# Sliding-window attention, two layers on one core: score units of two head groups by 256 queries, DMA transposes, bank pairs given out by the scheduler

## The chip, the core and the metric

The kernel runs on one NeuronCore of a Trainium2 chip. The core's engines work side by side, each in the order of its own instruction list: PE (TensorE, matmuls, with PEld its weight loads), ACT (ScalarE), DVE (VectorE), POOL (GpSimd) and SP (SyncE, which here only issues DMAs). PE writes to PSUM, eight banks of 512 f32 columns in 128 partitions; the other arrays lie in SBUF. The metric is the device time of one execution in microseconds.

## What is computed

x is 2048 rows of 512 (bf16). Two layers follow each other, each an attention block and a block that updates one row:

```python
x = x + A(layernorm(x))          # H = 32 heads of 16, window W = 256
    qkv = x @ wqkv
    scores = q k^T / 4; mask: 0 <= query - key < 256
    o = softmax(scores) v;  A = o @ wo
x = x + B(layernorm(x))          # B(x) = x + upd
    r = x @ w_r; idx = argmax(r)          # one row of 2048
    y = (silu(x[idx] @ w_gate) * (x[idx] @ w_up)) @ w_down
    upd[idx] = y * sigmoid(r[idx])
```

## The kernel before

The rows are worked on in tiles of 128, 16 a layer; both layers are one stream of 32 tiles, T = 0 to 31. Every operation is entered into a list with its engine, its reads and writes, an assumed duration and a priority (in units of a tile: `at` = T plus a fraction), and `Sched.schedule` plays the list through with these durations and writes down one fixed order for each engine. On the chip each engine follows its order and waits on semaphores; nothing is reordered there.

The steps of the stream, with their lines in the profile:

- `ln` makes the normalized tile XN (statistics on DVE, L516 and L517; the rest on POOL, L519 to L529), which PE transposes in eight pieces into PSUM (L546) and DVE copies to XNT (L554).
- For each batch of four tiles `qk` makes Q and K transposed for four groups of eight heads (L584; copies to QT and KTN, L603 and L605), and `vproj` makes V of each tile (L620, copy to VN, L627).
- `kscat` spreads K by eight DMAs for two tiles into the block-diagonal KBD (L639), `vscat` sends V through DRAM (`vd`, L648) into VBD by four DMAs (L654). These, the loads of x and the stores of the rows (`scr`, `out`) stand in SP's queue in the scheduled order.
- `attention` works on one tile of 128 keys. A unit is one of four head groups `s` by one of four blocks of 32 keys by the 288 queries that these keys can meet: two matmuls on the two halves of PE's rows, one for each bank of a pair (L682, four heads in each), then two small matmuls that add the mask, -30000, to the first and last 32 queries of the bank (L688), then one exponential on ACT over 2 x 288 columns into PT (L696). Units alternate between two bank pairs.
- The same function multiplies PT by VBD, with a column of ones for the denominators (L716, 192 matmuls a tile), into the pair ACC; DVE takes the reciprocal (L729, one a tile) and writes the normalized tile ON (L734).
- `out_proj` of tile T stands with tile T + 1: PE transposes ON (L546), DVE copies it to OT (L554), PE multiplies by WO (L750), DVE adds the residual (L755), and `mod_tile` makes the second normalization, the router value and the stores.
- All matmuls but the scores and PV share one pair, MISC.
- `select`, after 11 tiles of layer 0 and 12 of layer 1, finds the row: DVE reduces in each partition (L828 to L833), a DMA writes 128 pairs to DRAM (`vcd`, L834) and another reads them back into all partitions (BC, L835), DVE goes on (L837 to L848), then three DMAs gather the row. `mlp_gu` (L916) and `mlp_down` (L954) are its three products; the weights are loaded to MW in chunks of 0.9 MB. Whether the early choice held is checked at the end; where it did not, a second, plain kernel runs (it does not run here).

The pairs, and how a group is bound to one, are fixed in the code:

```python
ACC = 4
MISC = 6
...
                pair = 2 * (i % 2)
```

Of the kernel before, what the change touches and what calls it, by code (L numbers as in the profile page):

```python
# [56 lines left out]
class _Op:  # L57
    __slots__ = ("idx", "eng", "fn", "deps", "dur", "name", "is_dma", "prio", "signals", "count",
                 "dma_sem", "start", "end", "waits", "dma_extra", "force")

    def __init__(self, idx, eng, fn, deps, dur, name, is_dma, prio):
        self.idx = idx
        self.eng = eng
        self.fn = fn
        self.deps = deps
        self.dur = dur
        self.name = name
        self.is_dma = is_dma
        self.prio = prio
        self.signals = False  # L70
        self.count = 0
# [5 lines left out]
        self.force = None  # L77


class Sched:  # L80
# [6 lines left out]
    def __init__(self, dma_latency=2000.0, sem_latency=100.0, n_dma_slots=48):  # L87
# [7 lines left out]
        self.dma_ops = []  # L95
        self.base = 0.0
        self._vc_lookup = {}

    def add(self, eng, fn, reads=(), writes=(), banks=(), dur=100.0, name="", is_dma=False, prio=None, extra_deps=()):
# [13 lines left out]
        for b in banks:  # L113
# [11 lines left out]
        self.ops.append(op)  # L125
        for k in writes:
# [8 lines left out]
    def dma(self, queue, fn, reads=(), writes=(), nbytes=0, name="", prio=None, extra_deps=(), dur=None):  # L135
# [5 lines left out]
        op.dma_extra = nbytes / 150.0  # L141
# [8 lines left out]
    def schedule(self):  # L150
        ops = self.ops
        n = len(ops)
        users = [[] for _ in range(n)]
# [7 lines left out]
        for op in ops:  # L161
            if remaining[op.idx] == 0:
                _heappush(now[op.eng], (op.prio, op.idx))
        t_eng = {e: 0.0 for e in self.ENGS}
        order = {e: [] for e in self.ENGS}
        done = 0
        while done < n:
# [33 lines left out]
            done += 1  # L201
            for u in users[i]:
                remaining[u] -= 1
                uo = ops[u]
                rt = op.end + (self.sem_latency if self.needs_wait(uo, op) else 0.0)
                if rt > ready_time[u]:
                    ready_time[u] = rt
                if remaining[u] == 0:
                    ue = uo.eng
                    if ready_time[u] <= t_eng[ue]:  # L210
                        _heappush(now[ue], (uo.prio, u))
                    else:
                        _heappush(fut[ue], (ready_time[u], uo.prio, u))
# [16 lines left out]
    def analyze(self):  # L230
# [23 lines left out]
        while done < total:  # L254
# [12 lines left out]
            assert progressed, "deadlock in schedule order (cyclic wait)"  # L267

# [31 lines left out]
    def run_engine(self, e, handle, sems, dma_sems):  # L300
# [13 lines left out]
        if e == "sp":  # L314
# [5 lines left out]
            for slot, tot in sorted(totals.items()):  # L320
                handle.wait_ge(dma_sems[slot], tot)


ACC = 4
MISC = 6
NBATCH = 4
NS1 = 11
# [4 lines left out]
W = 288  # L332
# [3 lines left out]
class Builder:  # L336
# [16 lines left out]
    def alloc(self):  # L353
# [11 lines left out]
        self.XNT = self.sb("XNT", [128, 2, 4, 512], BF16)  # L365
# [11 lines left out]
        self.ONESB = self.sb("ONESB", [128, 128], BF16)  # L377
        self.ZEROB = self.sb("ZEROB", [128, 64], BF16)
        self.IDB = self.sb("IDB", [128, 128], BF16)
        self.II = self.sb("II", [128, 128], BF16)  # L380
        self.BM = self.sb("BM", [128, 2, 32], BF16)
# [15 lines left out]
        self.EQ = self.sb("EQ", [128, 128], F32)  # L397
        self.CAND = self.sb("CAND", [128, 128], F32)
        self.VC = self.sb("VC", [128, 2], F32)
        self.BC = self.sb("BC", [128, 128, 2], F32)  # L400
# [16 lines left out]
        self.VCD = nc.dram_tensor("vcd", [2, 128, 2], F32)  # L417
        self.uctr = 0
# [15 lines left out]
    def init(self):  # L434
# [12 lines left out]
        S.dma("act", lambda e: e.dma_start(self.WO[:], self.A_wo.rearrange("(kc p) n -> p kc n", p=128)), writes=["wo"], nbytes=512 * 1024, name="ld_wo", prio=-7.0)  # L447
# [4 lines left out]
        S.add(P, lambda e: e.memset(self.ONESB[:], 1.0), writes=["onesb"], dur=100)  # L452
        S.add(P, lambda e: e.memset(self.MHALF[:], -0.5), writes=["mhalf"], dur=60)
        S.add(P, lambda e: e.affine_select(out=self.IDB[:], in_=self.ONESB[:], pattern=[[-1, 128]], compare_op=ALU.is_equal,
                                           fill=0.0, base=0, channel_multiplier=1), reads=["onesb"], writes=["idb"], dur=300)
        S.base = -8.0
        S.add(P, lambda e: e.affine_select(out=self.M8[:], in_=self.ONESB[:, 0:8].rearrange("p (a h) -> p a h", a=2), pattern=[[-64, 2], [-16, 4]],
                                           compare_op=ALU.is_ge, fill=0.0, base=0, channel_multiplier=1), reads=["onesb"], writes=["m8"], dur=100)
# [3 lines left out]
        S.add(P, lambda e: e.memset(self.ZEROB[:], 0.0), writes=["zerob"], dur=100)  # L462
        S.add(P, lambda e: e.memset(self.II[:], 0.0), writes=["ii"], dur=100)
        S.add(P, lambda e: e.memset(self.BM[:], 0.0), writes=["bm"], dur=100)
        r = slice(0, 32)
        S.add(P, lambda e: e.affine_select(out=self.II[r, :].rearrange("p (a b) -> p a b", a=4), in_=self.ONESB[r, :].rearrange("p (a b) -> p a b", a=4),
                                           pattern=[[0, 4], [1, 32]], compare_op=ALU.is_equal, fill=0.0, base=0, channel_multiplier=-1),
              reads=["onesb"], writes=["ii"], dur=200)
        S.add(P, lambda e: e.affine_select(out=self.BM[r, 0, :], in_=self.ZEROB[r, 0:32], pattern=[[1, 32]], compare_op=ALU.is_ge,
# [1606 lines left out]
```

## Time and profile before

| | |
|---|---|
| runs (median, lowest, highest) | 434.2 us, 433.31, 435.35 |
| profiled execution | 433.42 us, of it 431.7 between first and last instruction |
| mean granted TensorE clock | 0.906 |
| first tile's reciprocal to the last's | 44.3 to 411.1 us |
| exponentials L696, 128x576 | 448, mean 651 ns |
| score matmuls L682, 128x288 | 896 |
| mask matmuls L688 | 1024 |
| PV matmuls L716 | 5760 |
| transposes L546 | 512 pieces of 64 columns |

A group's row names line, engine, operation, tiles and shape, then busy time and the mean of one instruction, then the engine's idle time just before them and what ended it. A mean holds an instruction's latency, part of which overlaps with its neighbours; for PE above all, spacing is read from starts in the timeline. In a row of the waits stand who waited, for whom, the us in total, the number of waits and the longest.

### The profile page before, as it was taken

To read this page: it belongs to the slowest core of one execution; us is meant where nothing else is said; L and a number is where in the kernel's file an instruction comes from. 1 tells how busy PE (TensorE), PEld (TensorE's weight loads), DVE (VectorE), ACT (ScalarE), POOL (GpSimd) and SP (SyncE) were. 2 spreads that over 40 slices of the span, in tenths; PEclk is the share of its full clock that TensorE was granted. 3 is DMA by queue.
4 is the path that set the end of the run, shared out by engine and by line. 5 is a ranking of instruction groups with operands and counts; after the bars stand their busy time and mean duration, and the time that the engine had idled before them with its cause. 6 is when DMAs were issued, how large, how long until landed. Compare 5 with 4: busy or idle time off the path is not lost.

```text
span 431.7 us, 22240 instructions
## 1 busy us (share of the span) xinstructions
PE 354.1 (82%) x10109; PEld 246.1 (57%) x10109; DVE 227.5 (53%) x551; ACT 295.8 (69%) x526; POOL 152.5 (35%) x373
## 2 busy tenths in 40 slices
PE   0598898799899999698699978899999998739862
PEld 0254566567666676457655556666766677517620
DVE  6773564347546655556355575466544555404441
ACT  2257788778988898765285858777988788845400
POOL 9963044324424352234314074243522132312040
PEclk9999999899999999989569999989999999956555
DMA  8704124222453233337741924423442243750600
GB/s 269 254 13 92 31 46 114 26 91 46 105 93 95 69 99 60 83 83 232 225 87 29 317 40 123 98 103 79 101 81 72 59 99 70 198 127 5 197 14 21
DMA packets 107023, 43.69 MB, mean 101 GB/s; under 512 B 82980, under 2 KB 101285, under 8 KB 106920
## 3 DMA queue, kind: packets, MB, share of 16 engines
q1 hardware_dynamic: 105432, 40.74, 36.5%
q8 instruction: 81, 1.33, 1.3%
q10 hardware_dynamic: 1488, 1.44, 1.1%
q14 instruction: 22, 0.18, 0.1%
HBM read 24.26 MB, written 13.96 MB: 89 GB/s over the span
## 4 chain that ended last, share of the span: by engine, by line
PE 53%; ACT 15%; DMA 10%; DVE 7%; SPq 6%; issue 5%; POOL 3%; DVEq 0%; ACTq 0%; POOLq 0%
ACT PT L696 14%; PE PS L584 13%; PE PS L682 11%; PE PS L716 9%; PE PS L750 7%; PE PS L620 6%; DMA vcd<-VC 4%; SPq L639 4%; PE PS L954 2%; DVE XR L755 2%; PE PS L688 2%; DMA KBD<-KTN 2%; DMA BC<-vcd 2%; PE PS L546 2%; PE PS L916 1%
## 5 line engine op out<-in xcount | busy, mean ns | idle before, releaser
L696 ACT ACTIVATE PT<-PS 128x576 bf16<-128x576 f32 (+5 forms) x512 | 287.0, 621 | 85.8 <-PE PS L688 82.4
L682 PE MATMUL PS<-QT,KBD 64*128 64x288 bf16 (+6 forms) x1024 | 146.6, 291 | 27.9 <-ACT PT L696 17.8
L716 PE MATMUL PS<-VBD,PT 64*128 64x34 bf16 x5760 | 116.2, 176 | 7.1 <-issue 4.4
L716 PEld LDWEIGHTS PS<-VBD,PT 64*128 64x128 bf16 x5760 | 97.5, 94 | 18.4 <-issue 10.2
L688 PE MATMUL PS<-BM,II 64*128 64x64 bf16 (+1 forms) x1024 | 100.5, 194 | 2.7 <-issue 2.7
L682 PEld LDWEIGHTS PS<-QT,KBD 64*128 64x128 bf16 x1024 | 52.0, 96 | 66.0 <-ACT PT L696 40.5
L777 POOL TENSOR_SCALAR RSM<-XR 128x1 f32<-128x1 f32 x32 | 9.3, 292 | 208.5 <-DVE XR L772 208.4
L584 PE MATMUL PS<-XNT,WQKV 64*128 64x512 bf16 x512 | 69.3, 396 | 3.3 <-DVE VN L627 2.2
L688 PEld LDWEIGHTS PS<-BM,II 64*128 64x128 bf16 x1024 | 52.4, 98 | 9.3 <-issue 2.2
L750 PE MATMUL PS<-WO,OT 64*128 64x256 bf16 x512 | 44.9, 300 | 2.0 <-DVE OT L554 0.7
L603 DVE CAST QT<-PS 128x512 bf16<-128x512 f32 x28 | 19.4, 692 | 48.5 <-PE PS L584 48.5
L755 DVE TENSOR_TENSOR XR<-PS,XR 128x512 f32<-128x512 f32 x32 | 22.1, 692 | 41.3 <-PE PS L750 39.9
L620 PE MATMUL PS<-WQKV,XNT 64*128 64x256 bf16 x512 | 40.4, 277 | 2.2 <-DVE XR L755 1.6
L584 PEld LDWEIGHTS PS<-XNT,WQKV 64*128 64x128 bf16 x512 | 22.0, 97 | 26.3 <-issue 4.2
L627 DVE CAST VN<-PS 128x512 bf16<-128x512 f32 x32 | 22.1, 692 | 15.3 <-PE PS L620 12.5
L750 PEld LDWEIGHTS PS<-WO,OT 64*128 64x128 bf16 x512 | 21.9, 102 | 11.4 <-DVE OT L554 2.6
L620 PEld LDWEIGHTS PS<-WQKV,XNT 64*128 64x128 bf16 x512 | 20.9, 95 | 10.7 <-DVE XR L755 3.4
L529 POOL TENSOR_SCALAR XN<-XR,RS 128x512 bf16<-128x512 f32 (+1 forms) x28 | 21.5, 769 | 10.1 <-PE PS L546 9.4
L605 DVE CAST KTN<-PS 128x512 bf16<-128x512 f32 x28 | 19.0, 678 | 10.8 <-DMA KBD<-KTN 10.8
L554 DVE COPY XNT<-PS 128x512 bf16<-128x512 bf16 x32 | 13.5, 421 | 21.2 <-PE PS L546 21.0
L734 DVE TENSOR_TENSOR ON<-PS,RD 128x256 bf16<-128x256 f32 x64 | 24.1, 414 | 0.4
L546 PE MATMUL PS<-IDB,XN 64*128 64x64 bf16 x256 | 10.0, 201 | 15.7 <-ACT XN L526 14.2
(101 smaller groups left out, 310.0 us busy)
## 6 DMA issues: line engine op xcount, KB each, us to landing
scr<-XR SPq DMA_DIRECT2D x13, 516.0 KB, 4.3
vd<-VN SPq DMA_DIRECT2D x16, 272.0 KB, 3.5
VBD<-vd SPq DMA_DIRECT2D x64, 68.0 KB, 2.8
XR<-scr SPq DMA_DIRECT2D x8, 512.0 KB, 4.4
KBD<-KTN SPq DMA_DIRECT2D x120, 32.0 KB, 2.9
MW<-in_B_w_gate_dram SPq DMA_DIRECT2D x4, 896.0 KB, 7.0
MW<-in_B_w_down_dram SPq DMA_DIRECT2D x4, 896.0 KB, 5.7
XR<-in_A_x_dram SPq DMA_DIRECT2D x8, 256.0 KB, 6.9
```

Of the source, the lines that this page charges most:

```text
L529: S.add("pool", lambda e: e.tensor_scalar(out=XN[:, k2, :], in0=x, scalar1=RS[:, k4, 1:2], scalar2=RS[:, k4, 2:3], op0=ALU.mult, op1=ALU.add),
L584: r = e.matmul(self.PS[:, bank + w, :], lhsT=self.WQKV[rows, j, 512 * w + 128 * s:512 * w + 128 * s + 128], rhs=XNT[rows, kb, j, :], start ...
L603: S.add("dve", lambda e: e.tensor_copy(out=self.QT[:, s, tok], in_=self.PS[:, MISC, :]), banks=[MISC], writes=["qt%d_%d" % (b % 4, s)], du ...
L620: r = e.matmul(o, lhsT=XNT[rows, kb, j, 128 * jt:128 * jt + 128], rhs=self.WQKV[rows, j, 1024 + 256 * w:1280 + 256 * w], start=(ph == 0 an ...
L627: S.add("dve", lambda e: e.tensor_copy(out=vout, in_=vin), banks=[MISC, MISC + 1], writes=["vn%d_%d" % (pr % 2, m2)], dur=650, name="evv")
L682: r = e.matmul(self.PS[:, pair + x, 0:n], lhsT=self.KBD[rows, k2, s, 4 * (T % 2) + b, :], rhs=self.QT[rows, s, q0:q0 + n], start=True, sto ...
L688: r = e.matmul(o, lhsT=self.II[rows, :], rhs=w, start=False, stop=True, skip_group_check=True)
L696: return e.activation(out=o, in_=self.PS[:, pair:pair + 2, 0:n], func=ACTF.Exp, scale=0.25)
L716: r = e.matmul(self.PS[:, ACC + x, 34 * gg:34 * gg + 34], lhsT=self.PT[rows, c:c + 128], rhs=self.VBD[rows, v3, b8, :, gg, :], start=st, s ...
L734: S.add("dve", lambda e, o=o, i0=i0, i1=i1: e.tensor_tensor(out=o, in0=i0, in1=i1, op=ALU.mult), reads=["rd%d" % t], banks=[ACC + x], writ ...
L750: r = e.matmul(self.PS[:, MISC + w, 0:256], lhsT=self.OT[rows, k2, j, :], rhs=self.WO[rows, j, 256 * w:256 * w + 256], start=(ph == 0 and ...
L755: S.add("dve", lambda e: e.tensor_tensor(out=self.xf(T).rearrange("p (x c) -> p x c", x=2), in0=self.PS[:, MISC:MISC + 2, 0:256], in1=self ...
```

## The change

- **Units.** A unit is now two head groups by 256 queries by 32 keys: four matmuls (L769) into a pair of banks, 2 x 256 columns in each, and one exponential over 1024 elements (L747). The last 32 queries of each block's window, the edge, are worked on in one further unit a tile: 32 matmuls of 32 columns (L798) and one exponential over 1024 elements. Eight full units and one edge unit a tile take the place of 16. The last two tiles of a layer have no edge unit, and shorter full units.
- **Masks by products.** The mask matmuls go. The exponentials of the first 32 queries are multiplied by a 0/1 mask MSK in place, by DVE twice a tile (L780, 512 elements), and those of the edge by POOL (L807, 1024 elements).
- **PV in two halves.** The function `pv` works on two of the four head groups at a time, with a group of banks, a reciprocal (L849) and a normalization (L851) of its own.
- **DMA transposes.** From the fifth tile on, XN goes to XNT two tiles at a time by a transposing DMA (L609, 14 of them), and ON to OT by one a tile (L860, 30; the last two tiles stay on PE). They are issued by SP. WO is loaded in an order that fits, by eight DMAs.
- **Bank pairs.** ACC, MISC and the alternation go. An operation belongs to a `Group` of a class: scores "s", others "m", the first four Q/K products "q". While it writes down the order, the scheduler gives a group that is ready one of four pairs that is free, with a limit for each class (`CAPS`).
- **Order.** Assumed latencies are by engine (`LAT`, a DMA's 2700 in place of 2000), the functions are called in order of an event list with finer times, and evictions have a higher priority (`URG`). KTN has two buffers, VN one in place of two.
- **Selection.** Two PE transposes bring the 128 pairs to one partition (L962), and DVE goes on there (L966 to L972). A 4-byte DMA out and back (`vcd`) remains for the check at the end.

```diff
-        self.KTN = self.sb("KTN", [128, 2, 4, 256], BF16)
+        self.KTN = self.sb("KTN", [128, 2, 2, 4, 256], BF16)
-        self.VN = self.sb("VN", [128, 2, 2, 4, 8, 17], BF16)
+        self.VN = self.sb("VN", [128, 2, 4, 8, 17], BF16)
...
+CAPS = {"s": 2, "m": 3, "q": 4}
+LEAD = 1.0
+URG = 1.0
-W = 288
+W = 256
...
+        def grant():
+            k = 0
+            while k < len(waiting) and pairs:
+                i = waiting[k][1]
+                g = ops[i].group
+                if held.get(g.cls, 0) >= CAPS[g.cls]:
+                    k += 1
+                    continue
+                del waiting[k]
+                held[g.cls] = held.get(g.cls, 0) + 1
+                pairs.sort()
+                t, g.bank, before = pairs.pop(0)
...
+        if g >= NBATCH:
+            if j % 2 == 1:
+                dst = self.XNT[:, kb, j - 1:j + 1].rearrange("p m j q -> p (m j) q")
+                S.dma("sp", lambda e: e.dma_start(dst, self.XN[:].rearrange("p m c -> p (m c)"), transpose=True), reads=["xn#0", "xn#1"],
+                      writes=["xnt%d_%d" % (kb, j - 1), "xnt%d_%d" % (kb, j)], nbytes=256 * 1024, name="dtrx", dur=1250, prio=at)
+            return
...
-                        r = e.matmul(self.PS[:, pair + x, 0:n], lhsT=self.KBD[rows, k2, s, 4 * (T % 2) + b, :],
-                                     rhs=self.QT[rows, s, q0:q0 + n], start=True, stop=False, skip_group_check=True)
...
-                        r = e.matmul(o, lhsT=self.II[rows, :], rhs=w, start=False, stop=True, skip_group_check=True)
...
+                for u in range(2):
+                    s = 2 * sp + u
+                    for x in range(2):
+                        rows = slice(64 * x, 64 * x + 64)
+                        r = e.matmul(self.PS[:, G.bank + x, W * u:W * u + n], lhsT=self.KBD[rows, k2, s, 4 * (T % 2) + b, :],
+                                     rhs=self.QT[rows, s, q0:q0 + n], start=(u == 0), stop=True, skip_group_check=True)
...
+        S.add("dve", lambda e: e.tensor_tensor(out=P, in0=P, in1=m, op=ALU.mult), reads=["msk"],
+              writes=["pt%d_%d" % ((4 * t + b) % 12, 2 * sp + u) for b in range(4) for u in range(2)], dur=380, name="mask", prio=at + 0.4 - URG)
...
+        S.add("pool", lambda e: e.tensor_tensor(out=P[:, :, :, 0:32], in0=P[:, :, :, 0:32], in1=m, op=ALU.mult), reads=["msk"], writes=key,
+              dur=1700, name="mask", prio=at + 0.2)
...
-        self.transposes(self.ON, k2, ["on#%d_%d" % (k2, i) for i in range(2)], "tro")
-        self.evict_t(self.OT[:, k2], "ot#%d" % k2, "evot")
+        if T < 2 * self.NT - 2:
+            S.dma("sp", lambda e: e.dma_start(self.OT[:, k2], self.ON[:, k2, :], transpose=True), reads=on, writes=["ot#%d" % k2],
+                  nbytes=128 * 1024, name="dtro", dur=1250, prio=at - 0.2)
+        else:
+            self.transposes(self.ON, k2, on, "tro", self.OT[:, k2], "ot#%d" % k2)
...
-        S.dma("sp", lambda e: e.dma_start(self.VCD[L], self.VC[:]), reads=["vc"], writes=["vcd%d" % L], nbytes=1024, name="vc_out")
-        S.dma("sp", lambda e: e.dma_start(self.BC[:].rearrange("p a b -> p (a b)"), self.VCD[L].rearrange("a b -> (a b)").partition_broadcast(128)),
-              reads=["vcd%d" % L], writes=["bc"], nbytes=128 * 1024, name="vc_in")
+            for c in range(2):
+                r = e.transpose(self.PS[0:1, G.bank, 128 * c:128 * c + 128], self.VC[:, c:c + 1], self.IDF[:])
```

Three places show what the order makes of it. First PE in the middle of layer 0, from a tile's score units to the projection of the tile before (L546 are its transposes, L750 the projection). Before:

```order
L682 MATMUL PS<-QT,KBD 128x288 x2
L688 MATMUL PS<-BM,II 128x2x32 x2
L546 MATMUL PS<-IDB,ON 128x64 x8
L716 MATMUL PS<-VBD,PT 128x34 x16
L682 MATMUL PS<-QT,KBD 128x288 x2
L688 MATMUL PS<-BM,II 128x2x32 x2
L750 MATMUL PS<-WO,OT 128x256 x8
```

And PE at such a place now, from the last PV of a tile (L833) to its projection (L872), with V's product (L701), full score units (L769, four matmuls each) and the edge unit (L798):

```order
L833 MATMUL PS<-VBD,PT 128x34 x80
L701 MATMUL PS<-WQKV,XNT 128x4x64 x8
L769 MATMUL PS<-QT,KBD 128x256 x8
L701 MATMUL PS<-WQKV,XNT 128x4x64 x8
L769 MATMUL PS<-QT,KBD 128x256 x8
L798 MATMUL PS<-QT,KBD 128x32 x32
L872 MATMUL PS<-WO,OT 128x256 x8
```

The transposes are gone from PE's row, and the projection stands behind four full units, one edge unit and V's product, counted from the last PV of its own tile.

Second, DVE in the selection of layer 1, from the last reduction within partitions to the step that goes on across them. Before (L837 reads BC, which the DMA brings):

```order
L833 TENSOR_REDUCE VC<-CAND 128x1
L554 COPY OT<-PS 128x2x4x64
L755 TENSOR_TENSOR XR<-PS,XR 128x512
L771 BN_STATS ST6M<-XR 128x6
L773 SCALAR_TENSOR_TENSOR JUNK,DOT<-XR,WR 128x512
L772 BN_AGGR XR<-ST6M 128x2
L837 TENSOR_REDUCE MT<-BC 128x1
```

Now (L966 reads what PE has transposed):

```order
L955 TENSOR_REDUCE VC<-CAND 128x1
L849 RECIPROCAL RD<-PS 128x16
L851 TENSOR_TENSOR ON<-PS,RD 128x256
L780 TENSOR_TENSOR PT<-PT,MSK 128x4x4x32
L966 COPY FROW<-PS 1x256
L967 TENSOR_REDUCE MT<-FROW 1x1
```

DVE's step across partitions now follows on PE in place of two DMAs, and three other operations stand between where there were five.

Third, PE at the end of the program, from the last PV to the matmul of the flag. Before (L954 are the down products):

```order
L716 MATMUL PS<-VBD,PT 128x34 x64
L546 MATMUL PS<-IDB,ON 128x64 x8
L750 MATMUL PS<-WO,OT 128x256 x16
L954 MATMUL PS<-MW,HT 1x512 x14
L1006 MATMUL PS<-ONESB,BADB 1x1
```

Now (L1050 are the gate and up products, L1091 the down products):

```order
L833 MATMUL PS<-VBD,PT 128x34 x96
L872 MATMUL PS<-WO,OT 128x256 x16
L1050 MATMUL PS<-XST,MW 128x1 x56
L1050 MATMUL PS<-XST,WQKV 128x1 x28
L1050 MATMUL PS<-XST,XNT 128x1 x28
L625 MATMUL PS<-IDB,ON 128x64 x8
L872 MATMUL PS<-WO,OT 128x256 x16
L1091 MATMUL PS<-MW,HT 1x512 x14
L1143 MATMUL PS<-ONEB,BADB 1x1
```

Behind the last PV there now stand the projection of the tile before and the gate and up products as well.

More of the change, by code (lines that the diff above doesn't have):

```diff
@@ L201, in schedule @@
             done += 1
+            g = op.group
+            if g is not None:
+                g.left -= 1
+                if g.left == 0:
+                    last = [j for j in g.ops if ops[j].eng != "pe"]
+                    pairs.append((max(ops[j].end for j in g.ops), g.bank, last))
+                    held[g.cls] -= 1
+                    grant()
             for u in users[i]:
@@ L607, in vproj @@
+        S.add("dve", lambda e: e.tensor_copy(out=self.KTN[:, kb, :, s, :], in_=k()), banks=[1], group=G, writes=["ktn%d_%d" % (kb, s)], dur=612, name="evk", prio=at - URG)
     def vproj(self, g, at):
```

599 lines of the change are left out of this document (339 added, 260 removed).

## The prediction

> **What bounds the kernel now.** I read the page's busy shares first, then the windows by stage, the groups by shape, the waits, and last a stretch of the timeline.
>
> ```profile
> span 431.7 us, 22240 instructions
> PE 354.1 (82%) x10109; PEld 246.1 (57%) x10109; DVE 227.5 (53%) x551; ACT 295.8 (69%) x526; POOL 152.5 (35%) x373
> 44.30:370.40 326.10, 291.50 (x8748) 207.77 (x8750) 179.79 (x432) 254.16 (x447) 111.43 (x278) 0.95 0.38 95
> 370.40:411.10 40.70, 28.24 (x944) 21.61 (x944) 14.18 (x47) 20.91 (x49) 6.54 (x18) 0.63 0.48 136
> 411.10:431.70 20.60, 8.91 (x39) 2.65 (x39) 6.68 (x23) 0.00 (x0) 4.33 (x10) 0.50 0.06 18
> L729 DVE RECIPROCAL RD<-PS x32: 340/357/359, 44.3 to 411.1; 128x32 f32<-128x32 f32 x32
> ```
>
> The window rows give PE, PEld, DVE, ACT and POOL busy, then the granted clock. No engine is full in the tile loop: PE 291.5 and ACT 254.2 of 326 us. The reciprocal L729 stands once at the end of each of the 32 tiles, so a tile takes (411.1 - 44.3) / 31 = 11.83 us. Ahead of it lie 44.3 us of start, behind it 20.6 us of tail at half clock.
>
> ```profile
> L696 ACT ACTIVATE PT<-PS 128x576 bf16<-128x576 f32 x60 | 35.2, 651 | 5.4 <-PE PS L688 5.1
> L696 ACT ACTIVATE PT<-PS 128x256 bf16<-128x256 f32 x8 | 3.1, 383 | 1.8 <-PE PS L688 1.7
> 307.69 3.37 ACT PT L696 x6
> ACT PT L696 <- PE PS L688: 82.4, 124, 4.3
> PEld PS L682 <- ACT PT L696: 40.5, 103, 5.0
> DVE MT L837 <- DMA BC<-vcd: 13.9, 2, 11.6
> DVE KTN L605 <- DMA KBD<-KTN: 10.8, 5, 3.6
> 372.90 11.36 DMA vcd<-VC
> 384.28 3.19 DMA BC<-vcd
> ```
>
> The first row is of the quiet window 120 to 160 us: 60 exponentials, 16 a tile, so 3.75 tiles in 40 us or 10.67 us a tile. The other 11.83 - 10.67 = 1.16 us a tile, 36 us over 31 tiles, are disturbances (the two selections, MLP loads, the seam of the layers). In the chain, six exponentials back to back take 3.37 us, 562 ns each, so ACT alone needs 16 x 562 = 8.99 us a tile. The waits show the loop between the two: ACT waits 82.4 us for scores, PE 40.5 us for ACT to free a score pair. DVE stands 13.9 us behind a DMA round trip, and works in order, so all behind it stands too.
>
> ```profile
> 130.12 0.29 PE L546 MATMUL PS<-IDB,ON 64*128 64x64 bf16 x8 [0.16 <-DVE KTN L605]
> 130.25 0.29 PE L682 MATMUL PS<-QT,KBD 64*128 64x288 bf16 x2
> 130.38 0.19 PE L688 MATMUL PS<-BM,II 64*128 64x64 bf16 x2
> 130.46 0.42 DVE L554 COPY OT<-PS 128x512 bf16<-128x512 bf16 x1 [0.39 <-PE PS L546]
> 130.84 0.19 PE L688 MATMUL PS<-BM,II 64*128 64x64 bf16 x2
> 130.87 0.36 PE L716 MATMUL PS<-VBD,PT 64*128 64x34 bf16 x16
> 131.08 0.60 PE L750 MATMUL PS<-WO,OT 64*128 64x256 bf16 x8
> 131.51 0.28 PE L682 MATMUL PS<-QT,KBD 64*128 64x288 bf16 x2
> 132.74 0.56 PE L716 MATMUL PS<-VBD,PT 64*128 64x34 bf16 x32
> 133.14 0.61 PE L620 MATMUL PS<-WQKV,XNT 64*128 64x256 bf16 x8
> 133.59 0.29 PE L682 MATMUL PS<-QT,KBD 64*128 64x288 bf16 x2
> 135.49 1.03 PE L584 MATMUL PS<-XNT,WQKV 64*128 64x512 bf16 x8
> 136.35 0.29 PE L682 MATMUL PS<-QT,KBD 64*128 64x288 bf16 x2
> ```
>
> Busy shares of PE hold pipeline latency, so I take starts. A score pair costs 130.38 - 130.25 = 0.13 us, a mask pair 130.87 - 130.84 = 0.03; 16 more PV matmuls cost 0.56 - 0.36 = 0.20 us, 12.5 ns each; eight of L750 0.43, of L620 0.45, of L584 0.86. A tile has 16 score and mask pairs (2.56), 192 PV matmuls (2.40), 16 each of L750 (0.86), L620 (0.90) and L584 (1.72), and 16 small transposes (0.20): 8.64 us. So the kernel runs at 10.67 quiet with ACT needing 8.99 and PE 8.64: neither bounds alone, their handing over does.
>
> **The change, part by part.** *Units.* Between 256 and 576 elements the mean of an exponential grows by (651 - 383) / 320 = 0.84 ns an element, so 1024 elements have a mean of 1026, less the overlap 651 - 562 = 89: 937 ns. Nine of them are 8.43 us a tile against 8.99: ACT gains 0.56. PE: score pairs of 256 columns cost 0.13 x 256 / 288 = 0.116, sixteen 1.85; the 32 edge matmuls at 12.5 ns, as the nearest narrow matmul, 0.40; the mask pairs and transposes go: 1.85 + 0.40 + 2.40 + 0.86 + 0.90 + 1.72 = 8.13 us, 0.51 less.
>
> The quiet idle, 10.67 - 8.99 = 1.68 us over 16 handovers, is 0.105 each. If it goes with the handovers, nine leave 0.95 and a tile takes 9.4; if it stays whole, 8.43 + 1.68 = 10.1. A unit of 937 ns covers the refill of the other pair better than one of 562, but the PE order is still fixed, so I take 9.7: 0.97 x 31 = **-30 us** (bounds -18 and -39).
>
> *Masks and evictions.* All are elementwise and priced by these rows.
>
> ```profile
> L554 DVE COPY OT<-PS 128x512 bf16<-128x512 bf16 x32 | 13.5, 423 | 14.4 <-PE PS L546 13.9 <-PE PS L688 0.2
> L734 DVE TENSOR_TENSOR ON<-PS,RD 128x256 bf16<-128x256 f32 x64 | 24.1, 414 | 0.4
> L529 POOL TENSOR_SCALAR XN<-XR,RS 128x512 bf16<-128x512 bf16 x12 | 9.2, 768 | 3.9 <-PE PS L546 3.6
> ```
>
> DVE gains 64 products of 512 elements, about 0.42 each, 27 us, and loses 58 copies of 0.42, 24 us; 64 short reciprocals take the place of 32. Its 227.5 us stay about 235, 60% of the new time: nothing on the path, and if the cover went, 0.42 us twice a tile between the last exponential and its PV. POOL gains 28 products of 1024 elements: 1.5 us by L529 at 768 for 512, 3.1 if the second input doubles it, so 43 to 86 us on 152.5; the edges are first read two tiles on, some 19 us, which hides it at either price.
>
> *DMA transposes.* Thirty ON to OT and fourteen XN to XNT go into SP's queue, of which no row shows one. Issue: bounds are the shortest and longest issue below; I take 1.25, between them. Landing: 2.2 to 8.7 by the same rows; I take 2.9, as the KBD scatter, SBUF to SBUF like these.
>
> ```profile
> KBD<-KTN SPq DMA_DIRECT2D x120, 32.0 KB, 2.9
> XR<-scr SPq DMA_DIRECT2D x8, 512.0 KB, 4.4
> L639 SPq DMA_DIRECT2D KBD<-KTN x120: 591/632/1930, 29.6 to 367.6; - x120
> L648 SPq DMA_DIRECT2D vd<-VN x16: 359/384/627, 31.0 to 370.8; - x16
> DMA to landing us min/median/max: 2.2/3.5/8.7
> ```
>
> SP issues two OT and one XNT in two tiles, 3.75 us beside some 9.8 (eight scatters at 0.63 to 0.77, four VBD loads, stores): 13.5 of 19.4 us, so the queue has room. Behind a waiting OT transpose stand the scatters and VBD loads; they are due a tile later. What the projection must now wait for is about 0.6 (the product into ON, a semaphore) + 1.25 + 2.9 = 4.75 us, against 0.76 us on chip before (130.12 to 130.88). In the new order PE has between the tile's last PV and its projection L872 sixteen of L701, four score units and one edge unit; ACT paces these five units at 0.937, 4.7 us. So it just fits: **0 us**, and each us beyond costs up to 30 us. The XNT pair has over a tile of slack, so it is hidden unless it is later than 8 us.
>
> Against this part the Trainium skill (VectorE: DVE Perf Modes, The three transpose paths) puts a 128x128 block at 390 ns on TensorE and 1309 ns through the DMA crossbar, and says to use TensorE if PSUM will do. By it the landing of four blocks is an estimated 5.2 us, the projection 2.3 us late, and the sum 69 us higher. No row here shows a crossbar transfer, and the matmul way is quicker than that page's (0.29 us for eight pieces of one tile).
>
> *Selection.* The two round trips vcd and BC leave DVE's path; two small PE transposes and a chain on one row take their place, under 3 us. *KTN* gets a second buffer, which ends the 10.8 us wait, and any free bank pair may now serve any group, which ends the queue for one pair. The MLP's loads and the layer seam stay. Of the 36 us of disturbances I take half, 13.9 + some 4 of the 10.8: **-18 us** (bounds 0 and -36).
>
> *Start and tail.* POOL's new mask building takes the place of the old; 0. At the tail the order puts the gate and up matmuls behind the last PV, with the projection of tile 30.
>
> ```profile
> 397.22 3.03 PE PS L916 x112
> 416.60 3.16 PE PS L954 x7
> 420.67 3.16 PE PS L954 x7
> ```
>
> That is 3.03 us more at half clock and up to 2.1 of the projection, while the two down groups no longer wait for one bank between them (420.67 - 419.76 = 0.9): **+3 us** (bounds 0 and +5).
>
> Sum against the profiled execution's 433.4 us (span 431.7; the median of the runs is 434.2, 0.8 above, which I leave out): 433.4 - 30 - 18 + 3 = **388 us**.
>
> **Rivals.**
> - *It goes only by the work that falls.* Idle stays whole (10.1 us a tile, -18), a third of the -18 comes (-6), tail +5: 414 us. For it: PE's order is written ahead, so each late transfer stops all behind it. Against: the longer unit.
> - *Everything fits.* -39 - 36 + 0: 358 us. For it: 8.43 of ACT and 8.13 of PE leave room for 9.4. Against: loads of 0.9 MB stay.
> - *The transposes are late; slower.* Place: PE before L872. Issue at 1.93 and landing at 4.4 as the 512 KB rows give 0.6 + 1.93 + 4.4 = 6.93 us, 2.2 beyond the 4.7 of cover; x 30 is 66 us: 454 us. It decides from 45 / 30 = 1.5 us, so from 6.2 us between ON and OT. For it: landings up to 8.7 us while others move. The page's price above gives 457.
> - *No change,* 434: the loop of exponential and score pair is untouched by the unit's size, and the lost DMA waits are met by new ones.
>
> **How the numbers follow.** 388 has 0.45 (its own range 372 to 402), 414 has 0.25, 358 has 0.16, no change 0.03, late transposes 0.11. The range 355 to 420 takes in the first three and leaves out about 2 in 10. About half a per cent is what a measurement of this kernel can tell from no change; faster by more than that 0.86, within it 0.03, slower 0.11.
>
> **What would show it.** Right: exponentials of 1024 elements spaced 0.94 us, a tile in 9.7 us by the reciprocals (now two a tile), ACT's wait for scores well under 82 us, no wait of DVE for vcd, and OT landing in about 3 us with no wait of L872 beyond 1 us. Wrong: PE waiting at L872 for OT, or for XNT at L659, SP's own queue waiting on ON with the scatters behind it, masks on POOL over 9 us a tile, or edge matmuls well over 12.5 ns.

## The result, and the profile after

The changed kernel takes 419.4 us (median of 4 runs, 415.17 to 422.07), against 434.8 of the kernel before beside it: a ratio of 0.9615, 95% interval 0.9532 to 0.9697. It is faster, by some 17 us where 46 were forecast; 388 is missed by 31 us, and 419.4 lies at the edge of the range. (Medians here are of all runs of a kernel; ratios are to the kernel before on the same chip and leave disturbed runs out.)

The profiled execution takes 415.17 us. Busy times, the windows (PE, PEld, DVE, ACT, POOL, granted clock, DMA share) and the reciprocals that end each half tile:

```profile
span 413.4 us, 20980 instructions
PE 316.3 (77%) x9521; PEld 224.8 (54%) x9521; DVE 243.4 (59%) x601; ACT 268.0 (65%) x298; POOL 219.9 (53%) x403
```

```profile
42.60:389.20 346.60, 282.22 (x9022) 205.72 (x9022) 206.03 (x511) 247.21 (x275) 180.05 (x314) 0.90 0.58 123
389.20:413.40 24.20, 11.04 (x159) 5.90 (x159) 9.89 (x39) 0.21 (x1) 7.32 (x20) 0.71 0.34 103
```

```profile
L849 DVE RECIPROCAL RD<-PS x64: 216/256/259, 36.1 to 389.2; 128x16 f32<-128x16 f32 x64
```

The first tile's second reciprocal is at 42.6, the last at 389.2: (389.2 - 42.6) / 31 = 11.18 us a tile, before 11.83. The loop gave 20.2 us, the start 1.7, and the tail took 3.6 back (24.2 against 20.6).

The ends of the tiles say where in the loop. The 29th tile's last reciprocal is at 370.4 us before and at 366.8 now, so the first 28 spacings take 326.1 and 324.2 us (319.5 in the second profile of the changed kernel, after_again), and the last three, in the stage of layer 1's selection, 40.7 and 22.4 (24.8 in after_again). A part of that is only order: 46 of 512 exponentials before and 22 of 284 now are left for these three. So the whole change gained 2 to 7 us in 28 tiles, and most of its gain lies at the end.

Waits (total, times, longest) and pieces of the chain:

```profile
ACT PT L747 <- PE PS L769: 93.1, 74, 11.9
DVE PT L780 <- ACT PT L747: 45.3, 31, 4.9
PEld PS L769 <- ACT PT L747: 34.3, 72, 1.2
PE PS L769 <- ACT PT L747: 15.1, 32, 0.7
PE PS L833 <- issue: 14.9, 15, 3.6
PE PS L872 <- DMA OT<-ON: 8.7, 4, 4.4
```

```profile
148.48 5.62 ACT PT L747 x6
...
131.35 0.63 SPq L1016
131.99 0.04 issue
132.03 8.41 DMA OT<-ON
```

```profile
L860 SPq DMA_TRANSPOSE OT<-ON x30: 1199/1310/3166, 43.3 to 378.3; - x30
...
DMA to landing us min/median/max: 2.4/4.0/8.8
```

Six exponentials back to back take 5.62 us, 937 ns each, as worked out; DVE's waits for vcd and KTN are gone. Yet ACT waits longer for scores (93.1 us against 82.4), though there are nine handovers a tile for sixteen. DVE's waits at the mask L780 and PE's for OT are new, and PE's waits for nothing that the profile shows ("issue") inside PV have grown from 4.4 to 14.9 us. The trace tells the landing of 23 of the 30 OT transposes: 20 took under 4.6 us from the start of the issue, three 7.9 to 8.8. Two of these three, the one shown above (8.41 us) and the longest, were issued right behind a load of MLP weights (L1016).

### Two rows that the prediction passed over

Granted clock and PE's rows at 102 to 120 us:

```profile
105.00:110.00 5.00, 3.34 (x149) 2.36 (x144) 4.61 (x13) 4.53 (x6) 3.90 (x9) 0.94 0.69 102
110.00:115.00 5.00, 3.80 (x42) 2.52 (x40) 1.05 (x2) 3.21 (x4) 4.84 (x9) 0.50 0.59 151
115.00:120.00 5.00, 4.50 (x166) 3.42 (x164) 3.80 (x9) 3.65 (x5) 2.13 (x5) 0.88 0.82 97
```

```profile
105.44 0.39 PE L769 MATMUL PS<-QT,KBD 64*128 64x256 bf16 x4 [0.38 <-ACT PT L747]
106.35 0.39 PE L769 MATMUL PS<-QT,KBD 64*128 64x256 bf16 x4 [0.52 <-ACT PT L747]
107.38 0.77 PE L833 MATMUL PS<-VBD,PT 64*128 64x34 bf16 x48 [0.64 <-DVE ON L851]
```

Three waits of 0.38 to 0.64 us come close together; from 109.4 the clock is 0.50 for 6.8 us, and only then full again. In the loop of the changed kernel 67 us are at half clock, before 60 (counted in windows of 1 us with a clock under 0.75). The Trainium skill (TensorE: Matmul & The Clock Gate, Part 1) lets the clock fall after an idle window of about 3.4 us. Here it falls with no wait over 0.64 us, and half clock covers 19% of the loop. The clock falls nine times in this loop. In the 3.4 us before, the longest gap between PE's starts (one that still runs is counted up to the fall) is 1.4 to 2.8 us in six of them and under 1 us in three, of which this is one; it is never 3.4.

The second row is "issue". PE's rows in one PV run:

```profile
209.33 0.97 PE L833 MATMUL PS<-VBD,PT 64*128 64x34 bf16 x56
213.93 0.35 PE L833 MATMUL PS<-VBD,PT 64*128 64x34 bf16 x12 [3.63 <-issue]
```

and the DMA queue in 211 to 213 us (packets, MB, share):

```profile
q8 instruction: 1, 0.02, 3.4%
```

PE stands for 3.63 us in the middle of PV without a semaphore; a block of instructions lands meanwhile. I measured all gaps of at least 0.7 us between PE's starts in the loop against the last landing on this queue. Of those without a wait, 15 (25.1 us) in the changed kernel and 10 (14.5 us) before, every one ends 1.26 to 2.03 us after a landing, most 1.3 to 1.5; gaps with a wait end anywhere from 0.1 to 7.8 us after. So these are fetches of PE's instructions that came late. The Trainium skill (Runtime: NRT & Kernel Launch, Instruction fetch mechanics) has this fetching hidden; in these traces it isn't. In the three longest gaps the transfer starts late, it isn't slow: the block of the gap above starts at 211.40, 1.28 us after PE's last start, and takes 1.08 us. In the changed kernel no two of the 77 fetches start less than 3.4 us apart. On average 247 instructions of PE go with one (2 x 9521 / 77), which PV, at 12.5 ns for two, would use up in an estimated 1.5 us.

### The profile page after: what moved, and what is told of

The parts are those of the page before. It is cut to its first block, busy times and chain, and to the rows that moved or that the text cites. A ratio compares the mean times of both kernels' runs of the same rounds, so it can differ in the third digit from the quotient of the medians.

```text
span 413.4 us, 20980 instructions
## 1 busy us (share of the span) xinstructions
PE 316.3 (77%) x9521; PEld 224.8 (54%) x9521; DVE 243.4 (59%) x601; ACT 268.0 (65%) x298; POOL 219.9 (53%) x403
## 3 DMA queue, kind: packets, MB, share of 16 engines
q8 instruction: 77, 1.26, 1.3%
## 4 chain that ended last, share of the span: by engine, by line
PE 50%; ACT 16%; DVE 12%; issue 8%; DMA 8%; POOL 2%; SPq 1%; DVEq 0%; POOLq 0%
ACT PT L747 16%; PE PS L833 13%; PE PS L659 11%; PE PS L769 9%; PE PS L872 8%; DMA OT<-ON 6%; PE PS L701 6%; DMA XR<-in_A_x_dram 2%; PE PS L798 2%; PE PS L1050 2%; DVE PT L780 1%; DVE JUNK L895 1%; DVE XR L877 1%; DVE ST6M L893 1%; DVE ON L851 1%
## 5 line engine op out<-in xcount | busy, mean ns | idle before, releaser
L747 ACT ACTIVATE PT<-PS 128x1024 bf16<-128x1024 f32 (+5 forms) x284 | 258.7, 999 | 96.0 <-PE PS L769 93.1
L833 PE MATMUL PS<-VBD,PT 64*128 64x34 bf16 x5760 | 103.2, 177 | 22.5 <-issue 14.9
L769 PE MATMUL PS<-QT,KBD 64*128 64x256 bf16 (+4 forms) x1024 | 100.6, 279 | 24.6 <-ACT PT L747 15.1
L833 PEld LDWEIGHTS PS<-VBD,PT 64*128 64x128 bf16 x5760 | 97.7, 94 | 39.2 <-issue 21.0
L807 POOL TENSOR_TENSOR PT<-PT,MSK 128x1024 bf16<-128x1024 bf16 x28 | 59.2, 2114 | 41.3 <-ACT PT L747 41.0
L769 PEld LDWEIGHTS PS<-QT,KBD 64*128 64x128 bf16 x1024 | 39.4, 97 | 54.1 <-ACT PT L747 34.3
L780 DVE TENSOR_TENSOR PT<-PT,MSK 128x512 bf16<-128x512 bf16 x64 | 30.8, 481 | 45.5 <-ACT PT L747 45.3
L872 PE MATMUL PS<-WO,OT 64*128 64x256 bf16 x512 | 46.7, 304 | 12.2 <-DMA OT<-ON 8.7
L701 PE MATMUL PS<-WQKV,XNT 64*128 64x256 bf16 x512 | 47.4, 297 | 4.1 <-issue 3.3
L872 PEld LDWEIGHTS PS<-WO,OT 64*128 64x128 bf16 x512 | 25.6, 104 | 22.2 <-DMA OT<-ON 9.6
L849 DVE RECIPROCAL RD<-PS 128x16 f32<-128x16 f32 x64 | 15.9, 249 | 34.0 <-PE PS L833 31.8
L659 PEld LDWEIGHTS PS<-XNT,WQKV 64*128 64x128 bf16 x512 | 25.1, 96 | 16.3 <-issue 4.8
L701 PEld LDWEIGHTS PS<-WQKV,XNT 64*128 64x128 bf16 x512 | 25.0, 102 | 13.7 <-issue 4.6
L851 DVE TENSOR_TENSOR ON<-PS,RD 128x256 bf16<-128x256 f32 x64 | 26.9, 420 | 1.2
L895 DVE SCALAR_TENSOR_TENSOR JUNK<-XR,WR 128x512 bf16<-128x512 f32 x32 | 24.6, 768 | 0.0
L589 DVE BATCH_NORM_STATS2 ST<-XR 128x6 f32<-128x512 bf16 (+1 forms) x32 | 20.9, 672 | 2.9 <-DMA XR<-in_A_x_dram 2.9
```

Source lines behind the costliest of these rows:

```text
L659: r = e.matmul(self.PS[:, G.bank + w, :], lhsT=self.WQKV[rows, j, 512 * w + 128 * s:512 * w + 128 * s + 128], rhs=XNT[rows, kb, :, j, :], ...
L701: r = e.matmul(o, lhsT=XNT[rows, kb, jt, j, :], rhs=self.WQKV[rows, j, 1024 + 256 * w:1280 + 256 * w], start=(ph == 0 and j == 0), stop=(p ...
L747: return e.activation(out=out, in_=i, func=ACTF.Exp, scale=0.25)
L769: r = e.matmul(self.PS[:, G.bank + x, W * u:W * u + n], lhsT=self.KBD[rows, k2, s, 4 * (T % 2) + b, :], rhs=self.QT[rows, s, q0:q0 + n], s ...
L780: S.add("dve", lambda e: e.tensor_tensor(out=P, in0=P, in1=m, op=ALU.mult), reads=["msk"], writes=["pt%d_%d" % ((4 * t + b) % 12, 2 * sp + ...
L807: S.add("pool", lambda e: e.tensor_tensor(out=P[:, :, :, 0:32], in0=P[:, :, :, 0:32], in1=m, op=ALU.mult), reads=["msk"], writes=key, dur= ...
```

## Experiments

### The DMA transposes

One thing holds for all that follows. half_exps, half_projections, half_both, scores_twice and fewer_pv change the work and leave every engine's order as it is in the changed kernel; half_both_pe does so beside all_tr_on_pe, and before_half_both beside the kernel before. Every other version is planned anew, so its time holds the edit and a new order together, and no run separates the two.

all_tr_on_pe moves both kinds back to TensorE, ot_on_pe only ON to OT; ot_planned_late keeps them and has the planner expect ON to OT later.

```
-  if g >= NBATCH:                   +  if g >= 10 ** 6:       # XN to XNT on PE
-  if T < 2 * self.NT - 2:           +  if T < 0:              # ON to OT on PE
   name="dtro", dur=1250, prio=at - 0.2                        # ot_planned_late: + late=4000.0
```

> The changed kernel once more, unaltered, so that the runs beside it have a partner on the same chip. Every theory expects 415 to 422 us, tile 11.0 to 11.3 us by the second reciprocals (42.6 to 389.2 in the first profile), waits at L872 for OT of 5 to 12 us and a landing of OT of 8 us at the longest.

Measured: 420.1 us, ratio 0.9681 (0.9580 to 0.9782), the partner of the next three.

> Both kinds of transposes go back to TensorE with a copy by DVE; all else is as in the changed kernel. Theory A (the DMA transposes land late, hold PE at the projection and load the DMA rings, and that is where most of the missing gain went): the 18 us of waits at L872 and the 10 to 15 us of new gaps of PE without a wait go, while PE gets 16 small transposes a tile (0.2 us x 32 = 6 us): 390 to 402 us. Theory B (the waits are those of a PE order written ahead, whatever moves the tiles; a late transpose only takes the place of another wait): 413 to 424 us, with the time of L872's waits found again at other waits of PE. Theory C (PE and DVE need the room that the DMA transposes make): slower than the changed kernel, 425 to 435 us, as 64 copies of 0.42 us (27 us) come back to DVE.

Measured: 413.1 us, 0.9504 (0.9451 to 0.9558). Against the two ratios of the changed kernel the transposes cost 1.1 to 1.8%, 5 to 8 us, and not the 18 to 28 of theory A. This version beats the kernel before, and the changed kernel beside it by intervals that just miss each other.

> Only ON to OT goes back to TensorE; XN to XNT stays a DMA transpose. Theory A: the wait at L872 is all that matters of the transposes' latency, so this takes most of what both together take: 395 to 408 us, with no wait of PE for OT above 1 us. If the load on the rings counts rather than the latency, one third of the DMA transposes' bytes stays, and the time lies between the changed kernel and the one with both on TensorE. Theory B: 413 to 424 us.

Measured: 420.9 us (413.88 to 425.28), too scattered for an interval. Even the lowest of its six times lies above theory A's 395 to 408. Taking ON to OT back alone gained nothing that can be seen.

> The DMA transposes stay; only the planner's landing time for ON to OT is raised to 4.0 us, so that it puts the projection L872 later in PE's written order. Theory A with latency as the cause: waits at L872 fall from 18 us (PE and its weight loads) to under 4 and the time to 400 to 410 us. Theory A with the load on the rings as the cause: L872's wait falls, the gaps of PE without a wait stay, 410 to 417 us. Theory B: 413 to 424 us, the wait turns up at another place.

Measured: 428.7 us, 0.9885 (0.9827 to 0.9942). PE's matmuls now wait 0.6 us for OT in place of 8.7, and it is 2% slower than the changed kernel: what a wait shows is not what taking it away brings. The edit is stronger than the expectation says: `late` is added to what the planner already assumes (2.7 us and 0.9 for the bytes), so it plans a landing 7.6 us after the issue, not 4.0. The order that this asks for costs more than the waits did. That a smaller delay would gain nothing is not shown.

The same transposes in the kernel before (both through SP's queue, all else as it was):

```
-  self.transposes(self.ON, k2, ..., "tro"); self.evict_t(self.OT[:, k2], ...)
+  S.dma("sp", lambda e: e.dma_start(self.OT[:, k2], self.ON[:, k2, :], transpose=True), ...)   # and XN to XNT, two tiles at a time
```

> The kernel before with the two kinds of DMA transposes alone. Theory A, which gives them the shortfall: 445 us or more, as the wait for OT falls into a fuller PE stream. The first run with both back on TensorE took 7 us less than the changed kernel, so theory B expects a like loss here: 434 to 445 us. If they are hidden, as the prediction took it: 430 to 435 us.

Measured: 439.6 us, 1.0089 (1.0012 to 1.0166): +4 us. PE's waits for OT are there too:

```profile
PEld PS L761 <- DMA OT<-ON: 9.5, 8, 3.1
PE PS L761 <- DMA OT<-ON: 6.5, 5, 2.8
```

### The selection alone

In the kernel before, the two round trips are replaced by the two PE transposes and the chain on one row:

```
-  S.dma("sp", lambda e: e.dma_start(self.VCD[L], self.VC[:]), ...)
-  S.dma("sp", lambda e: e.dma_start(self.BC[:]..., self.VCD[L]...partition_broadcast(128)), ...)
+  r = e.transpose(self.PS[0:1, MISC, 128 * c:128 * c + 128], self.VC[:, c:c + 1], self.IDF[:])   # c = 0, 1; then DVE on row 0
```

> The kernel before with the selection alone changed: two small PE transposes and a chain on one row in place of the round trips through memory. The prediction gave this 13.9 us: 420 to 423 us. If it is what the whole change brought: 414 to 420 us. If the stall is only renamed: 430 us or more.

Measured: 429.0 us, 0.9795 (0.9733 to 0.9858): -9 us, and no wait of DVE for vcd is left.

### Masks and score pairs

```
-  S.add("dve", ... op=ALU.mult ... name="mask" ...)     # no_dve_masks
-  S.add("pool", ... op=ALU.mult ... name="mask" ...)    # no_masks: this one too
-  CAPS = {"s": 2, "m": 3, "q": 4}
+  CAPS = {"s": 3, "m": 3, "q": 4}                       # three_score_pairs
```

> The changed kernel without the 64 mask products L780 on DVE (part of the computation is left out: the diagonal blocks are not masked). Theory E (the masks put a wait for the exponential into DVE's queue, 45.3 us in 31 waits, and the evictions and reciprocals behind it are late, so PE and ACT are): the time falls to 392 to 402 us, ACT's wait for scores from 93 to under 70 us. Theory B (PE's written order; what is late merely changes its name): 412 to 420 us. If only the 31 us of the products' own work counts, 405 to 412 us.

Measured: 420.6 us, 0.9664 (0.9599 to 0.9730): nothing. In the order planned without them, the largest new wait of DVE and 31 us of its work were worth nothing that can be seen.

> As before, and without POOL's 28 edge products L807 (59 us of POOL) too: nothing is masked in the main pass. Theory E with POOL's share: below the one without DVE masks by 5 us or more. If POOL's masks are hidden, as the prediction held (read two tiles on), within 3 us of the one without DVE masks.

Measured: 414.5 us, 0.9547 (0.9475 to 0.9619): at most 6 us below the changed kernel, within the intervals. The prediction's 0 for the masks holds to within these 6 us.

> The scheduler may give score units three of the four bank pairs in place of two. Theory F (ACT and PE wait for each other because only two score pairs are in flight; the 1.68 us of idle a tile is the refill): ACT's wait for scores falls from 93 us to under 60 and the time to 395 to 408 us. Theory B, or if the fourth pair is needed by the other matmuls: 415 to 430 us.

Measured: 435.0 us, 0.9998 (0.9924 to 1.0072). A third pair for the scores cost 3%, and ACT's wait for scores rose to 103.9 us. The pair is taken from the other matmuls, so this shows that giving it to the scores doesn't help, not that pairs are plentiful.

### Taking work from ACT and PE

These versions leave work out. First half_exps and half_projections:

```
-  return e.activation(out=out, in_=i, ...)
+  return e.activation(out=out[:, :, :, 0:n // hv], in_=i[:, :, :, 0:n // hv], ...)   # hv = 2 from tile 3 on
...
+  q = 128 if j in (0, 3) else 16       # L659; in L701 and L872 likewise
-  rhs=XNT[rows, kb, :, j, :]
+  rhs=XNT[rows, kb, :, j, 0:q]
```

> The changed kernel in which, from the fourth tile on, each exponential covers half of its columns (the rest of the probabilities is left out); the order on every engine is the same. By 0.84 ns an element an exponential falls from 0.937 to about 0.51 us, ACT from 8.4 to 4.6 us a tile. If ACT sets the pace and the stalls of PE are hidden beside it: 330 to 350 us. If the two wait for each other by turns: PE's waits for ACT, 34 + 15 + 8 = 57 us, go at most, so 360 to 390 us. If PE with its own stalls and half clock sets the pace alone: 400 us or more.

Measured: 413.2 us, 0.9420 (0.9360 to 0.9479): 2 to 3% below the changed kernel for a third of ACT's busy time. ACT does not set the pace, and it doesn't set it by turns with PE either, by the bounds that were given for that (360 to 390).

> The changed kernel with half of the contraction of the three projections L659, L701 and L872 left out (their middle matmuls shrink to an eighth of the columns); the order is the same. PE's work falls from 8.1 to about 6.8 us a tile, some 41 us in all. If PE with its stalls sets the pace: 378 to 390 us. If the two wait for each other by turns: 390 to 405 us. If ACT sets it: 408 us or more.

Measured: 410.7 us, 0.9390 (0.9325 to 0.9455): 2 to 3% for some 41 us of PE by the prices of the prediction (its busy time, more of it now at half clock, falls from 316.3 to 291.5). PE's work alone does not set it.

half_both makes both edits, half_both_pe adds the two of all_tr_on_pe, before_half_both makes them in the kernel before, and half_both_no_masks is half_both_pe without the mask products of no_masks.

> Half of the columns in the exponentials and half of the contraction of the projections left out together, same order. Theory B (ACT and PE hold the pace by turns, so that either alone keeps it): 345 to 375 us. Theory T (a third thing paces: the order's waits for DMA and DVE, the fetching of PE's instructions): 395 to 412 us. Theory D (the clock): PE idles more, its clock falls to half for over 110 us of the loop and gives back most of what was taken; between 375 and 400 us.

Measured: 403.8 us, 0.9229 (0.9149 to 0.9309): only 4 to 5% below the changed kernel, for some 41 us of PE and over 90 us of ACT (its busy time falls from 268.0 to 175.5). That is in theory T's range. Shares of the chain by engine, half_both:

```profile
PE 36%; DVE 18%; DMA 16%; issue 9%; POOL 7%; SPq 6%; ACT 6%; POOLq 0%; DVEq 0%
```

> As half_both (half of the exponentials' columns and half of the projections' contraction left out), but with both transposes on TensorE. Theory A2 (the DMA transposes are the third thing: with them the loop cannot run faster than about 11 us a tile, whatever ACT and PE do): 350 to 380 us, against 404 with them. Theory T2 (the third thing is the rest: DVE's and SP's written order, the loads, the scatters, fetching): 395 to 405 us.

Measured: 397.1 us, 0.9098 (0.9029 to 0.9167): the same 4% below all_tr_on_pe. The DMA transposes are not what keeps it there either.

> The kernel before with the same work left out (half of the columns of the exponentials from the fourth tile on, half of the contraction of its three projections). If its loop was paced by ACT and PE, as the prediction read it: 360 to 385 us, that is more than 50 us off, where the changed kernel gave 16. If it had the same floor: 415 to 428 us.

Measured: 411.5 us, 0.9444 (0.9373 to 0.9515), 24 us off: a little below the 415 to 428 given for a floor, and far from 360 to 385. The kernel before had such a floor already.

> As half_both_pe, and without the 64 mask products on DVE (31 us of it) and the 28 on POOL (59 us). If DVE or POOL in their written order are the floor: 365 to 382 us. If PE's own gaps at no wait and its half clock are: 390 to 398 us, with gaps at no wait still over 40 us and half clock over 80 us of the loop.

Measured: 390.1 us, 0.8901 (0.8843 to 0.8960), 2% below half_both_pe. The waits of PE without a releaser grew to:

```profile
PEld PS L831 <- issue: 43.5, 37, 5.7
PE PS L831 <- issue: 36.7, 27, 5.6
```

All 27 gaps of at least 0.7 us without a wait (49.4 us) end 1.20 to 1.53 us after a block of instructions landed. So late fetches are the largest part of PE's gaps that is left here. That they are the floor is not shown, as no run takes them away from this kernel; half clock, at 73 us, was under the 80 expected.

### Clock and fetch

pv_spread_pe stands on all_tr_on_pe, the other two on the changed kernel.

```
-  for u in range(2):            +  for u in (0, 1, 0, 1):                                # scores_twice
-  for kb in blocks:             +  for kb in (blocks if st or last else blocks[:1]):     # fewer_pv
-  prio=at + 0.02 * part - PVL   +  prio=at + 0.09 * part - PVL                           # pv_spread_pe
```

> Each of the eight score units of a tile makes its matmuls twice into the same place (the result stays the same): 1.86 us of PE a tile more, 59 us in all, same order. Theory D (PE idles too much and pays with half clock): the half-clock time of the loop falls from 67 us to under 40 and the time stays within 415 to 432 us. If PE's work sets the pace at its own price: 450 us or more.

Measured: 448.0 us, 1.0271 (1.0190 to 1.0353): +26 to 29 us for 59 us of work. Granted clock of this run and of half_projections, where the work goes the other way (the changed kernel: 0.901):

```profile
core 0: 445.2 us, clock 0.935
```

```profile
core 0: 409.3 us, clock 0.842
```

More work, higher clock; less work, lower clock. Theory D has the sign, but the time misses its 415 to 432: the clock returns a part, not all.

> A third of the PV matmuls L833 is left out (64 of 192 a tile: 0.8 us of PE and 128 of its instructions a tile), same order. Theory G (fetching instructions holds PE inside the PV runs, 18 to 25 us in the changed kernel): those gaps fall by half or more and the time to 395 to 405 us, more than half_projections gave for one and a half times the PE time. If PE's work alone counts: 410 to 416 us.

Measured: 410.4 us, 0.9383 (0.9305 to 0.9460). Gaps without a wait of at least 0.7 us fell from 25.1 us to 2.9, so they come and go with PV's instructions. But theory G's time (395 to 405) failed: it went no further than half_projections', as waits took their place (those of PE's matmuls for OT rose from 8.7 to 18.8 us).

> Both transposes on TensorE, and the six parts of a PV unit are given priorities 0.09 apart in place of 0.02, so that other matmuls stand between them. Theory G (the new units bunch PV in runs of 64 to 96 matmuls of 12.5 ns, which take instructions faster than they are fetched; 18 to 25 us of PE's gaps stand inside these runs with no wait): the gaps at L833 fall under 10 us and the time from 413 to 398 to 406 us. Theory B: 410 to 420 us.

Measured: 415.8 us, 0.9468 (0.9410 to 0.9526), as all_tr_on_pe. PV matmuls in runs of 64 and more fell from 1952 to 1216 of 5760, but such gaps rose from 21.1 to 34.8 us. How long a run is, then, is not what makes a fetch late; what is stays open.

### The loop of these runs side by side

In us, worked out from each profiled execution (which lies up to 5 us off the kernel's median: 415.2 against 419.4 for the changed kernel, 418.4 against 413.2 for half_exps; so a few us between two rows say little): the loop from the first tile's last reciprocal to the last tile's; the gaps of at least 0.3 us between PE's starts, with and without a semaphore wait; time at half clock.

| kernel (profiled execution) | loop | gaps, wait | gaps, no wait | half clock |
|---|---|---|---|---|
| before (433.4) | 366.8 | 43 | 20 | 60 |
| before_half_both (410.7) | 346.4 | 48 | 42 | 76 |
| after (415.2) | 346.6 | 64 | 34 | 67 |
| scores_twice (447.0) | 375.1 | 41 | 40 | 42 |
| half_exps (418.4) | 346.5 | 46 | 45 | 89 |
| half_projections (411.1) | 343.3 | 93 | 35 | 107 |
| fewer_pv (413.4) | 345.0 | 96 | 20 | 98 |
| half_both (405.8) | 338.2 | 84 | 41 | 111 |
| all_tr_on_pe (411.4) | 348.8 | 59 | 25 | 58 |
| half_both_pe (400.3) | 338.7 | 63 | 47 | 88 |
| half_both_no_masks (394.2) | 328.3 | 48 | 60 | 73 |

What is taken from PE comes back in large part as gaps and half clock. From before to after, the loop outside the gaps fell from 304 to 249 us, and the gaps rose from 63 to 98. From after to half_projections it fell to 215, the gaps rose to 128 and half clock by 40 us: the loop gained 3.

## Why the prediction was wrong, step by step

- *Bound: "neither bounds alone, their handing over does".* This step failed. The durations were right (937 ns an exponential; four score matmuls 0.22 to 0.24 us; 32 edge matmuls 0.40 us), but the idle time is not set by the handing over of ACT and PE: fewer handovers left ACT waiting 93 us, and without half of the exponentials' and of the projections' work the time fell by 24 us before and by 16 to 20 after. In half_both a tile still takes 10.9 us, where by the prices some 6.8 of PE and 4.6 of ACT are left. What the runs show in its place is a sum of late instructions, half clock, and waits of five fixed orders for DVE and transfers. In these runs, where one of them shrank, another mostly grew; what each is worth alone stays open.

The window on which the prediction read its quiet idle needs a word of its own:

```profile
120.00:160.00 40.00, 37.97 (x1179) 27.45 (x1175) 24.61 (x57) 34.63 (x60) 16.76 (x43) 1.00 0.35 81
```

Here the clock is full and no late fetch is seen: PE's gaps of at least 0.3 us come to 3.0 us, each with a wait, and ACT's waits for scores to 5.1 us, most of the 1.68 us a tile. So the waits were read rightly. But before_half_both, with half of that work left out, runs 60 exponentials in the same 40 us, and its idle grows instead: ACT waits 13.6 us, and PE has 5.6 us of gaps without a wait. Waits of two engines for each other don't show that the two set the pace.

- *Pace, -30.* Mis-sized by that reading. The forecast is 0.97 us a tile; over the first 28 tiles the two profiles of the changed kernel gained 0.07 and 0.24, with the cost of the DMA transposes in it. No run has the units alone. The units with KTN's buffer, the shared pairs and the new order are what stands between before_pe_select and all_tr_on_pe: 0.9795 to 0.9504, 2.9% or 13 us, where the sum has 30 and some 4.
- *Selection, 13.9 of the -18.* Measured 9 us, alone.
- *DMA transposes, 0.* The sum 0.6 + 1.25 + 2.9 counts the issue twice, as a row's landing time runs from the start of the issue (the OT transpose issued at 132.03 lands 8.41 us after that). From there the forecast is 4.15 us and the measured median 4.0, of it 1.31 for the issue: right by luck. The three landings of 7.9 to 8.8 us were not in it. PE's list has only four waits at L872; the transposes cost 5 to 8 us by all_tr_on_pe and 4 in the kernel before. The rule of the Trainium skill weighed there (VectorE: DVE Perf Modes, Rules for kernel authors), to use TensorE where PSUM will do, was right in its direction; the 69 us estimated from that page were not.
- *Masks, 0.* Held, though POOL's product took 2.11 us and DVE stood 45 us at L780. *Tail +3:* 3.6. *Start 0:* -1.7.

The steps -9, -13 and +8 (with after_again's ratio) add up to that ratio, 0.9681, whatever their causes: the middle one is a remainder, not a measurement of its own. Of the rivals, "it goes only by the work that falls" (414) came nearest, at 0.25. Its ground, that each late transfer stops PE's fixed order, is a part of what the runs show; its number is luck in part, since its -18 for the units isn't in the tiles, and the selection alone gave 9 where it takes 6.

## What to carry to other kernels

Before an idle time is given to two engines that wait for each other, take a good part of the work from both: if the time hardly moves, a lighter unit will not shorten it. Read the granted clock and the waits on nothing in the loop beside the named waits, because work taken from PE may return there. And do not price a wait by its length: the run with nearly no wait for OT was slower, and the run without the 45 us of mask waits was the same, each in an order of its own.

## What the runs showed of the hardware

- Half clock followed waits of under 0.7 us each, three within some 3 us, and lasted 6.8 us. Nine times the clock fell in the changed kernel's loop, never after a gap of PE as long as 3.4 us.
- A PV matmul of 34 columns costs 12.5 ns and is two instructions with its weight load; in such runs a late fetch of a 16 KB block stops PE until mostly 1.2 to 1.6 us after it lands. No two of the changed kernel's fetches start less than 3.4 us apart. The 77 blocks of the changed kernel took a median of 1.05 us each and 2.08 at most, the 81 before 0.97 and 1.79.
- A 128x512 DMA transpose in SBUF took a median of 1.31 us to issue and landed 2.4 to 8.8 us after the issue began, with a median of 4.0.
